# Fixed PSUM banks, whole-bank masked copies and small score products in a linear-attention and feed-forward kernel

## The chip, the cores and the metric

The kernel runs on one core of one Trainium2 chip. The metric is device time in microseconds (us), lower is better. Before the change it is 613.46 us, the median of three runs (613.08 to 613.84). The engines are TensorE (PE, matrix products, with its weight loads PEld), VectorE (DVE), ScalarE (ACT), GpSimd (POOL), and SyncE (SP), which issues DMAs.

## The reference

Two blocks follow each other. The first is a recurrence over time with a decay per channel, for 4 sequences, 8 heads, 768 steps and heads of 48 channels; the second is a feed-forward layer with SiLU from 384 to 2048 and back, on all 3072 tokens, in float32.

```python
for t in range(S):
    cur = np.einsum('bhd,bhe->bhde', u[None] * kt, vt)
    y[:, :, t] = np.einsum('bhd,bhde->bhe', rt, state + cur)
    state = wt[:, :, :, None] * state + np.einsum('bhd,bhe->bhde', kt, vt)
...
x = y.transpose(0, 2, 1, 3).reshape(B * S, H * D)
h = x @ w_in
out = (h * (1.0 / (1.0 + np.exp(-h)))) @ w_out
```

## The kernel before

The work is cut into 12 units: 6 pieces of 128 time steps, each for two pairs of sequences. Within a unit the recurrence is done as scores: a lower triangular matrix of 128 x 128 per head and sequence, which multiplies the values. The triangle is filled in seven levels, l = 0 to 6. At level l, blocks of c = 2^l steps meet in pairs, and the later block of a pair reads the earlier one. Queries (`tr`) and keys (`tk`) are multiplied by decay products between levels: `grow_queries` (L607, on DVE) and `grow_keys` (L625, on POOL), with copies by `odd_keys` (L595, on ACT). From unit 2 on, `prepare` makes a second `tr` (L762 and L764), so that two levels can be multiplied in one go by `burst`. The diagonal comes from `bonus` steps (L430 to L447, later L487 and L521), which are written into `score` by L584 or L557.

A level's products, `score_products`, exist in two forms. The whole form (L694) multiplies, for each of four head pairs p and two heads e, all 128 key steps with the 128 query entries of the level, of which only some lie inside blocks. The small form (L686) multiplies only the parts that are needed: 64 x 64, for level 5 32 x 32. Products with e = 0 and e = 1 go to two PSUM tiles. `keep_masked` (L704) then copies a whole tile of 128 x 512 into `score` under a mask; for small products `keep_level` copies pieces, under masks on DVE (L792, 64 x 128 each, eight a level) or, for levels 5 and 6, plainly (L785), where the first half of level 6 is done by DVE and the rest by ACT. In `scores`, used by units 0 and 1 and by two levels of unit 2, some halves are copied by ACT (L723).

Small products are used from unit 2 on, for levels from `APART` = 3 up. Units 4 and later begin at level 2 with the bonus work on blocks of eight steps, so they multiply only levels 3 to 6; unit 3 has levels 1 to 6.

[...]

After the scores, `turn_apart` (L812) and `turn_k` (L820) turn the keys back, `y_state` (L836) and `y_values` (L844; L857 in units 0 and 1) multiply state and scores into y, L849 copies it out, and `update` (L871, L885) advances the state. The feed-forward layer of a unit runs one or two units later: `up` (L979) in eight groups, each followed by the SiLU on ACT (L988, result `gt`), `sums` (L1027, on DVE) and seven products `quarter` (L1045), each evicted by L1052 or L1054. For units 0 and partly 1, `down` (L1001) is used. In the first 100 us the weights are also rounded, in pieces that pass ACT (L209, L211, L217), DVE (L228, L229) and POOL (L241).

The order is written by hand. Each engine executes its instructions in the order in which the lists of steps at the end of the kernel issue them: units 0 and 1 level by level with the weight pieces between, unit 2 in four lists, and units 3 to 11 by the groups of `mix`, with steps of the feed-forward layer put between groups.

Of the kernel before, what the change touches and what calls it, by code (L numbers as in the profile page):

```python
# [8 lines left out]
F32 = mybir.dt.float32  # L9
# [29 lines left out]
def kernel(  # L39
# [11 lines left out]
    nc = tc.nc  # L51

    B, H, S, D = r.shape
    DM, DF = moe_w_in.shape
    L = 128
    NL = 7
    NB = 2
    NP = H // 2
# [17 lines left out]
    pt = ctx.enter_context(tc.tile_pool(name="pt", bufs=2))  # L76
    ps = ctx.enter_context(tc.tile_pool(name="ps", bufs=1, space=bass.MemoryType.PSUM))
    ctx.enter_context(tc.manual_schedule())


    raw = const.tile([128, NSLOT, 3, NB, H, PD], F32, name="raw")
# [283 lines left out]
    def turn_in(i, s, name):  # L365

        flat = raw[:, i % NSLOT, WRK[name]].rearrange("p b h d -> p (b h d)")
        p_tr = ps.tile([128, NP, NB, L // 2], F32, name="p_m", bufs=2)
        for p in range(NP):
            for e in range(2):  # L370
                at = ((2 * p + e) * 2 + s) * D
                nc.tensor.matmul(p_tr[PD * e:PD * e + PD, p].rearrange("p b i -> p (b i)"), lhsT=flat[:, at:at + PD],
                                 rhs=ident, start=(p == 0), stop=(p == NP - 1))
        turned[i, s, name] = p_tr
# [21 lines left out]
    def reverse_v(i):  # L396
        flat = vq[i].rearrange("p h d -> p (h d)")
        if i < NTOK:
            p_v = ps.tile([128, H * D], F32, name="p_m", bufs=2)
            nc.tensor.matmul(p_v, lhsT=mirror, rhs=flat, start=True, stop=True)  # L400
            nc.scalar.copy(out=flat, in_=p_v)
            return
        nc.vector.stream_shuffle(out=flat, in_=flat, mask=list(range(31, -1, -1)))
# [157 lines left out]
    def bonus_spread(i):  # L561

        if i < NTOK:
            if i == 0:
                diag[i] = p_w[:, 0, 0:NB * H * 2].rearrange("p (b h s) -> p b h s", b=NB, h=H)
            else:
                diag[i] = ps.tile([128, NB, H, 2], F32, name="p_m", bufs=2)
            for b in range(NB):
                for s in range(2):
                    nc.tensor.matmul(diag[i][:, b].rearrange("p h s -> p (h s)"), lhsT=spread[:, s, b, :],  # L570
                                     rhs=own_sums[:, s].rearrange("p h s -> p (h s)"), start=(b == 0 and s == 0),
                                     stop=(b == NB - 1 and s == 1))
            return
        both_b = pt.tile([128, NB, H, 2], F32, name="both_b", bufs=1)
        nc.scalar.copy(out=both_b[:, 0], in_=diag[i][0])
        for g in range(4):
            nc.scalar.copy(out=both_b[(3 - g) * 32:(4 - g) * 32, 1], in_=diag[i][1][g * 32:(g + 1) * 32])
        nc.vector.stream_shuffle(out=both_b[:, 1], in_=both_b[:, 1], mask=list(range(31, -1, -1)))
        diag[i] = both_b
# [76 lines left out]
        start_keys(i, nc.gpsimd, False)  # L656


    APART = FIRST

    def dims_of(have, start, *dims):
        return bass.AP(tensor=have.tensor, offset=have.offset + start, ap=[have.ap[0], *dims])

# [5 lines left out]

    def score_products(i, l, queries, sc):  # L670
        c, ni = 1 << l, L >> (l + 1)
        if i >= NTOK and l >= APART:
            for p in range(NP):
                for x in range(4 if c == 32 else 2):
                    for e in range(2):
                        rows = slice(PD * e, PD * e + D)
                        if c >= 32:
                            b, first = corner(l, x)
                            q = (p, 2 * NP - 1 - p)[b]
                            to, have = sc[e][x * c:(x + 1) * c, q, first // 2 * c:(first // 2 + 1) * c], queries[rows, q, (first + 1) * c:(first + 2) * c]  # L680
                        else:
                            apart = 2 * (NP - p) - 1
                            to = dims_of(sc[e][x * 64:(x + 1) * 64, p, :], 32 * x, [apart * L // 2 + 32 - 64 * x, 2], [1, 32])
                            have = dims_of(queries[rows, p, :], 64 * x + c, [apart * L + 64 - 128 * x, 2], [2 * c, 32 // c], [1, c])
                        m = 32 if c == 32 else 64
                        nc.tensor.matmul(to, lhsT=tk[i][rows, X[l % 2] + p, x * m:(x + 1) * m], rhs=have, start=True, stop=True)  # L686
            return
# [19 lines left out]
    def scores(i, l, *between):  # L707
        c, ni = 1 << l, L >> (l + 1)

        name = "p_h" if i == 0 and l % 2 == 1 else "p_sc"  # L710
        sc = [ps.tile([128, Q, L // 2], F32, name=name, bufs=2) for e in range(2)]
        score_products(i, l, tr[i], sc)
        if i < NTOK and l + 2 < NL:
            odd_keys(i, l + 1)
# [52 lines left out]

    def burst(i, l):

        other = (second[0], "p_o") if i == NTOK else (ps, "p_m")  # L770
        for x, (pool, name) in enumerate(((ps, "p_sc"), other)):
            made[i, l + x] = [pool.tile([128, Q, L // 2], F32, name=name, bufs=2) for e in range(2)]
        score_products(i, l, before.pop((i, l)), made[i, l])
        score_products(i, l + 1, tr[i], made[i, l + 1])

    def keep_level(i, l):
        c = 1 << l
        for e in range(2):
            if l < APART:
                keep_masked(i, l, e, made[i, l])  # L780
                continue
            for x in range(4 if c == 32 else 2):
                if c >= 32:
                    b, first = corner(l, x)
                    (nc.vector.tensor_copy if (l, e) == (NL - 1, 0) else nc.scalar.copy)(  # L785
                        out=score[x * c:(x + 1) * c, i % NSC, e, b * NP:(b + 1) * NP, (first + 1) * c:(first + 2) * c],
                        in_=made[i, l][e][x * c:(x + 1) * c, b * NP:(b + 1) * NP, first // 2 * c:(first // 2 + 1) * c])
                    continue
# [16 lines left out]

    def turn_apart(i):

        apart[i] = [ps.tile([128, NB, NP, D], F32, name="p_sc" if i < NTOK else "p_m", bufs=2) for e in range(2)]
        for x in range(Q):
            for e, to in enumerate(apart[i]):  # L810
                rows = slice(PD * e, PD * e + D)
# [15 lines left out]
    def y_state(i):  # L827

        n, b0 = units[i]
        for e in range(2):  # L830
            p_yt[i, e] = ps.tile([128, NP, L], F32, name="p_m", bufs=2)
        for p in range(NP):
            for b in range(NB):
                for e in range(2):
# [15 lines left out]

    def y(i, b):

        p_yt[i, b] = ps.tile([128, NP, L], F32, name="p_h" if i == 0 else "p_m", bufs=2)
        for p in range(NP):
            for e in range(2):
                h = 2 * p + e
# [6 lines left out]
    def update(i, b):  # L863
# [1 line left out]
        if n == S // L - 1:  # L865
            return
        if b == 0:
            p_kv[i] = ps.tile([128, NB, NP, D], F32, name="p_m" if i < NTOK else "p_sc", bufs=2)
        for p in range(NP):
            for e in range(2):  # L870
                nc.tensor.matmul(p_kv[i][PD * e:PD * e + D, b, p, :], lhsT=kq[i, b][:, p, PD * e:PD * e + D],  # L871
# [17 lines left out]
    def dense_x(i, b):  # L889

        if b == 0:
            xt[i] = pt.tile([128, KC, TU], F32, name="xt", bufs=1)
        p_x = ps.tile([128, KC, L], F32, name="p_h" if i == 0 else "p_m", bufs=2)
        for x, (c, p) in enumerate(parts):
            nc.tensor.matmul(p_x[:, c, :], lhsT=dense[:, x, :], rhs=yt[i][:, p, b, :],
                             start=(x == 0), stop=(x == len(parts) - 1))
# [99 lines left out]
    def down(i, b, part, parts=4):  # L996
        n, b0 = units[i]
        if part == 0:
            po[i, b] = ps.tile([128, DM], F32, name="p_m", bufs=2)
        for f in range(part * FC // parts, (part + 1) * FC // parts):  # L1000
            nc.tensor.matmul(po[i, b], lhsT=gt[i, f // 2][:, f % 2, b * L:(b + 1) * L], rhs=w_out_sb[:, f, :],  # L1001
                             start=(f == 0), stop=(f == FC - 1))
# [72 lines left out]

    def beat(n):

        p = ps.tile([128, L], F32, name="p_m", bufs=2)
        for x in range(n):
            nc.tensor.transpose(p, ident, ident)  # L1080

# [108 lines left out]
```

## Time and profile before

| | |
|---|---|
| median of three runs | 613.46 us |
| profiled execution | 613.64 us |
| its span, first to last instruction | 611.9 us |
| PE busy | 597.9 us (98%) |
| DVE busy | 441.6 us (72%) |
| POOL busy | 361.3 us (59%) |
| ACT busy | 226.2 us (37%) |
| L694, whole products | 256 instructions, 272 ns each at the median |
| L686, small products | 1600 instructions, 211 to 218 ns each at the median |
| L704, masked copy of a whole tile | 29, 690 to 729 ns each at the median |
| L792, masked copy of a piece | 160, 290 to 294 ns each at the median |
| L785 on DVE / on ACT, half of level 6 in pieces of 64 x 256 | 20 of 0.42 us / 20 of 0.37 us |

The busy rows add up each engine's instructions; the span is 1.7 us shorter than the time of the execution. Each product in float32 shows as two instructions. Products overlap within PE, so what a level costs PE is read from the starts of what comes before and after, not from the duration of one instruction. A line of waits names who waited for whom, with total, count and longest in us. In lists by time the first two columns are start and duration; a bracket at the end gives idle time of that engine before the instruction and who ended it. A line by stretch gives, for each engine, busy time and instruction count.

### The profile page before, as it was taken

How to read it: one execution, taken by the hardware profiler on the slowest of the kernel's cores; microseconds unless marked ns; L12 is line 12 of the kernel's file. 1: busy time of each engine (PE TensorE's matmuls, PEld its weight loads, DVE VectorE, ACT ScalarE, POOL GpSimd, SP SyncE). 2: the span in 40 equal slices, each digit the busy share in tenths (PEclk: the TensorE clock that was granted, in tenths of full speed). 3: DMA queues.
4: the chain of work that ended last, by engine and by line, in shares of the span. 5: the costliest groups of instructions: out<-in, count | busy, mean ns of one | idle time of the engine just before them, and what ended most of it. 6: DMA issues, size and time to landing. Idle time of an engine off the chain costs nothing.

```text
span 611.9 us, 14906 instructions
## 1 busy us (share of the span) xinstructions
PE 597.9 (98%) x5790; PEld 534.0 (87%) x5790; DVE 441.6 (72%) x849; ACT 226.2 (37%) x496; POOL 361.3 (59%) x414
## 2 busy tenths in 40 slices
PE   9999999999998998999999999999999999999997
PEld 8788876698798888889889889989989989989997
DVE  7879779899795697687687687587678677761041
ACT  6788883331430440351351341241241242241110
POOL 6998478556578278378478468558658648500000
PEclk9999999999999999999999999999999999999999
DMA  9967773353543643543543552453362322101000
GB/s 225 291 142 196 147 226 46 55 115 49 120 64 52 129 67 55 122 70 53 116 74 54 108 83 51 92 98 53 71 118 51 54 74 53 35 2 27 27 0 27
DMA packets 203079, 53.43 MB, mean 87 GB/s; under 512 B 186752, under 2 KB 194816, under 8 KB 203008
## 3 DMA queue, kind: packets, MB, share of 16 engines
q1 hardware_dynamic: 201424, 51.88, 41.4%
q8 instruction: 46, 0.75, 0.5%
q10 hardware_dynamic: 1584, 0.59, 0.4%
q14 instruction: 25, 0.20, 0.1%
HBM read 43.21 MB, written 5.24 MB: 79 GB/s over the span
## 4 chain that ended last, share of the span: by engine, by line
PE 76%; DVE 9%; SPq 3%; POOL 3%; DMA 3%; issue 2%; ACT 2%; POOLq 0%; DVEq 0%; ACTq 0%
PE p_h L979 35%; PE p_o L1045 28%; SPq L109 3%; DMA tokens_w<-in_w_dram 2%; PE p_m L844 2%; DVE temps L1027 2%; PE p_sc L686 2%; POOL tk L625 2%; PE p_sc L694 2%; PE p_m L1001 1%; PE p_m L686 1%; DVE tr L607 1%; PE p_m L836 1%; DVE score L792 1%; DVE block_sums L521 1%
## 5 line engine op out<-in xcount | busy, mean ns | idle before, releaser
L979 PE MATMUL p_h<-xt,w_in_sb 128*128 128x256 f32 x1152 | 258.9, 382 | 1.8 <-ACT gt L988 1.1
L979 PEld LDWEIGHTS p_h<-xt,w_in_sb 128*128 128x128 f32 x1152 | 215.9, 190 | 33.2 <-ACT gt L988 1.2
L988 ACT ACTIVATE gt<-p_h 128x512 f32<-128x512 f32 x90 | 53.6, 596 | 194.3 <-PE p_h L979 194.0
L625 POOL TENSOR_TENSOR tk<-tk,tw 128x256 f32<-128x256 f32 x128 | 89.9, 724 | 49.1 <-issue 22.9
L1045 PE MATMUL p_o<-own,temps 128*128 128x192 f32 x528 | 88.9, 327 | 4.8 <-DVE temps L1054 4.8
L1045 PEld LDWEIGHTS p_o<-own,temps 128*128 128x128 f32 x528 | 85.9, 190 | 6.2 <-DVE temps L1054 6.0
L1045 PE MATMUL p_o<-w_out_sb,gt 128*128 128x192 f32 x508 | 87.4, 328 | 0.0
L1045 PEld LDWEIGHTS p_o<-w_out_sb,gt 128*128 128x128 f32 x508 | 82.7, 190 | 0.9 <-issue 0.4
L487 POOL TENSOR_TENSOR ruk<-tokens_rk 128x768 f32<-128x768 f32 (+1 forms) x32 | 48.1, 1512 | 52.7 <-DMA tokens_rk<-in_k_dram 40.1
L1027 DVE TENSOR_TENSOR temps<-gt 128x256 f32<-128x256 f32 x84 | 57.5, 684 | 19.8 <-ACT gt L988 19.8
L408 POOL TENSOR_TENSOR tw<-tw 128x256 f32<-128x256 f32 (+6 forms) x83 | 43.9, 529 | 37.2 <-DVE tw L360 33.3
L595 ACT COPY tk<-tk 128x256 f32<-128x256 f32 x52 | 21.0, 403 | 101.5 <-POOL tk L625 72.2
L607 DVE TENSOR_TENSOR tr<-tr,tw 128x512 f32<-128x512 f32 x61 | 52.5, 860 | 4.3 <-POOL tk L625 1.0
L1054 DVE TENSOR_TENSOR partial<-p_o,partial 128x192 f32<-128x192 f32 x33 | 11.8, 356 | 35.7 <-PE p_o L1045 35.3
L1027 DVE TENSOR_TENSOR temps<-temps,gt 128x256 f32<-128x256 f32 x43 | 31.3, 729 | 1.5
L1054 DVE TENSOR_TENSOR temps<-p_o,partial 128x192 f32<-128x192 f32 x22 | 7.9, 358 | 32.2 <-PE p_o L1045 22.7
L1045 PE MATMUL p_o<-w_out_sb,temps 128*128 128x192 f32 x176 | 30.4, 326 | 0.0
L1045 PEld LDWEIGHTS p_o<-w_out_sb,temps 128*128 128x128 f32 x176 | 28.9, 190 | 0.0
L849 ACT COPY yt<-p_m 48x512 f32<-48x512 f32 x40 | 23.2, 580 | 14.9 <-DMA raw<-in_k_dram 7.2
L487 POOL TENSOR_TENSOR spare<-tokens_rk 128x384 f32<-128x384 f32 (+1 forms) x16 | 28.5, 1783 | 0.0
L521 DVE TENSOR_REDUCE block_sums<-ruk 128x4 f32<-128x192 f32 (+1 forms) x48 | 24.1, 542 | 3.6 <-POOL ruk L487 3.6
L634 POOL TENSOR_TENSOR tk<-tk,tw 128x256 f32<-128x256 f32 x32 | 26.2, 839 | 0.0
(186 smaller groups left out, 864.1 us busy)
## 6 DMA issues: line engine op xcount, KB each, us to landing
w_out_sb<-in_moe_w_in_dram SPq DMA_DIRECT2D x6, 768.0 KB, 7.8
w_out_sb<-in_moe_w_out_dram SPq DMA_DIRECT2D x4, 768.0 KB, 5.5
own<-in_moe_w_out_dram SPq DMA_DIRECT2D x4, 768.0 KB, 5.9
tokens_rk<-in_r_dram SPq DMA_DIRECT2D x8, 384.0 KB, 4.5
tokens_rk<-in_k_dram SPq DMA_DIRECT2D x8, 384.0 KB, 5.4
tokens_w<-in_w_dram SPq DMA_DIRECT2D x8, 384.0 KB, 6.3
xt<-yt SPq DMA_DIRECT2D x60, 48.0 KB, 2.0
raw<-in_w_dram SPq DMA_DIRECT2D x80, 32.0 KB, 2.4
```

The costliest lines, as they stand in the source:

```text
L408: engine.tensor_tensor(out=up, in0=t[:, :, 0::2], in1=t[:, :, 1::2], op=ALU.mult)
L487: mul = lambda out, one, two: nc.gpsimd.tensor_tensor(out=out, in0=one, in1=two, op=ALU.mult)
L521: add = lambda out, have: nc.vector.tensor_reduce(out=out, in_=have, axis=mybir.AxisListType.X, op=ALU.add)
L595: nc.scalar.copy(out=keys(i, X[(l + 1) % 2] * L + c, [4 * c, blocks], [c, 2], [1, c]), in_=keys(i, NP * L + c, [4 * c, blocks], [NP * L + ...
L607: nc.vector.tensor_tensor(out=odd, in0=odd, in1=tw[i][l][:, :, 0::2][:, :, :, None].to_broadcast([128, Q, L >> (l + 1), c]), op=ALU.mult)
L625: nc.gpsimd.tensor_tensor(out=out, in0=have, in1=odd_products(i, l, b, *blocks), op=ALU.mult)
L634: nc.gpsimd.tensor_tensor(out=have, in0=have, in1=odd_products(i, l, b, [2, NP * ni]), op=ALU.mult)
L849: nc.scalar.copy(out=yt[i][PD * e:PD * e + D, :, b, :], in_=p_yt[i, e][PD * b:PD * b + D])
L979: nc.tensor.matmul(p_h[:, a, :], lhsT=w_in_sb[:, c, f * 128:(f + 1) * 128], rhs=xt[i][:, c, :], start=(c == 0), stop=(c == KC - 1))
L988: nc.scalar.activation(out=gt[i, m], in_=p_h, func=AF.Silu)
L1027: nc.vector.tensor_tensor(out=out, in0=one, in1=two, op=op)
L1045: nc.tensor.matmul(p, lhsT=left(f), rhs=right[:, f, :], start=(f == 0), stop=(f == FH - 1))
```

## The change

1. `p_m` and `p_sc` are no longer asked from the pool at each use: two tiles of a whole bank each are made once, and a function `bank` hands them out in turn, with the shape that the user wants.
2. Small products are used wherever the unit is not the first (`i > 0`), at all levels, and at level 6 of the first unit.
3. Because a kept bank holds defined data in every place, masked copies may read a whole bank though only parts were just written. So `keep_level` uses `keep_masked` for level 3 and, after unit 2, for level 4 (and 1 and 2 as before). Level 4 of unit 2, whose products lie in `p_o`, keeps the pieces.
4. The first half of level 6 is copied by ACT in place of DVE.

```diff
+    banks = {name: [ps.tile([128, 512], F32, name=f"{name}{x}") for x in range(2)] for name in ("p_m", "p_sc")}
+    turns_of = {name: 0 for name in banks}
+
+    def bank(name, *dims):
+        have = banks[name][turns_of[name] % 2][:]
+        turns_of[name] += 1
+        steps, n = [], 1
+        for d in dims[::-1]:
+            steps.insert(0, [n, d])
+            n *= d
+        return bass.AP(tensor=have.tensor, offset=have.offset, ap=[have.ap[0], *steps])
...
-            p_v = ps.tile([128, H * D], F32, name="p_m", bufs=2)
+            p_v = bank("p_m", H * D)
...
-    APART = FIRST
...
     def score_products(i, l, queries, sc):
         c, ni = 1 << l, L >> (l + 1)
-        if i >= NTOK and l >= APART:
+        if i > 0 or l == NL - 1:
...
-        name = "p_h" if i == 0 and l % 2 == 1 else "p_sc"
-        sc = [ps.tile([128, Q, L // 2], F32, name=name, bufs=2) for e in range(2)]
+        odd = i == 0 and l % 2 == 1
+        sc = [ps.tile([128, Q, L // 2], F32, name="p_h", bufs=2) if odd else bank("p_sc", Q, L // 2) for e in range(2)]
...
     def burst(i, l):
-        other = (second[0], "p_o") if i == NTOK else (ps, "p_m")
-        for x, (pool, name) in enumerate(((ps, "p_sc"), other)):
-            made[i, l + x] = [pool.tile([128, Q, L // 2], F32, name=name, bufs=2) for e in range(2)]
+        made[i, l] = [bank("p_sc", Q, L // 2) for e in range(2)]
+        made[i, l + 1] = [second[0].tile([128, Q, L // 2], F32, name="p_o", bufs=2) if i == NTOK else bank("p_m", Q, L // 2) for e in range(2)]
...
     def keep_level(i, l):
         c = 1 << l
         for e in range(2):
-            if l < APART:
+            if c < 32 and (i > NTOK or l == FIRST):
                 keep_masked(i, l, e, made[i, l])
                 continue
             for x in range(4 if c == 32 else 2):
                 if c >= 32:
                     b, first = corner(l, x)
-                    (nc.vector.tensor_copy if (l, e) == (NL - 1, 0) else nc.scalar.copy)(
+                    nc.scalar.copy(
```

The other uses of `p_m` and `p_sc` change as `p_v` does.

## The prediction

> **What bounds the kernel now.** I read the page first, then busy time by stretches, the waits of PE, and the timeline around each place that the change touches. The busy row:
>
> ```profile
> PE 597.9 (98%) x5790; PEld 534.0 (87%) x5790; DVE 441.6 (72%) x849; ACT 226.2 (37%) x496; POOL 361.3 (59%) x414
> ```
>
> PE works for 597.9 of 611.9 us, so time taken from PE counts unless another engine takes its place at that spot. Busy time by stretches, columns PE, PEld, DVE, ACT, POOL, shows where that is near:
>
> ```profile
> 36.40:66.00 29.60, 29.53 (x226) 24.42 (x227) 26.27 (x33) 27.32 (x41) 25.33 (x28) 1.00 0.65 167
> 66.00:100.00 34.00, 34.00 (x242) 27.32 (x240) 26.49 (x32) 25.53 (x38) 22.00 (x21) 1.00 0.71 173
> 100.00:149.00 49.00, 47.17 (x524) 38.74 (x524) 46.15 (x79) 13.76 (x35) 32.79 (x34) 1.00 0.41 71
> 149.00:190.00 41.00, 38.15 (x406) 33.99 (x397) 36.38 (x67) 13.48 (x34) 26.83 (x30) 1.00 0.44 83
> 190.00:240.00 50.00, 47.88 (x490) 43.57 (x489) 37.60 (x72) 14.70 (x36) 32.09 (x38) 1.00 0.45 81
> 240.00:550.00 310.00, 309.03 (x3174) 280.92 (x3174) 228.84 (x467) 98.09 (x242) 193.40 (x221) 1.00 0.39 71
> ```
>
> From 36 to 66 (unit 1's levels, woven with unit 0's first layer) all engines are nearly full; from 100 to 149 DVE is full 46.15 of 49; after 240 PE has no gap to speak of. Where PE stood idle:
>
> ```profile
> PE p_o L1045 <- DVE temps L1054: 4.8, 4, 2.1
> ...
> PE p_o L686 <- DVE tr L762: 1.1, 1, 1.1
> PE p_h L979 <- ACT gt L988: 1.1, 1, 1.1
> ...
> PE p_m L694 <- POOL tk L625: 0.7, 1, 0.7
> ```
>
> The four waits of L1045 are at 187 (1.76), 236 (2.12), 374 (0.38) and 423 (0.59). The other three are at 116, 162 and 139.
>
> [...] A whole level and a pair of small levels:
>
> ```profile
> 50.05 1.16 PE L694 MATMUL p_sc<-tr,tk 48*128 48x128 f32 x16
> 51.14 2.86 PE L979 MATMUL p_h<-xt,w_in_sb 128*128 128x256 f32 x12
> ```
> ```profile
> 148.38 0.69 PE L686 MATMUL p_sc<-tr,tk 48*64 48x64 f32 x32
> 148.89 0.65 PE L686 MATMUL p_m<-tr,tk 48*64 48x64 f32 x32
> 149.47 10.63 PE L979 MATMUL p_h<-xt,w_in_sb 128*128 128x256 f32 x48
> ```
>
> Start to start, the whole level holds PE for 51.14 - 50.05 = 1.09 us with 16 instructions; two small ones hold it for 149.47 - 148.38 = 1.09, the first 0.51, the second, with the change back to a full array, 0.58.
> [...]
> [...]
>
> **The change, part by part.**
> (a) *Kept banks.* The names p_m and p_sc alternate between two tiles as before, in the same order of users. Before, a new tile waits until all users of the one two turns back are done; now the first writer waits for the bank's last readers, which are the same instructions. Cost taken: 0. The bounds: 0 to 0.1 us a level, by one or two more 51 ns waits; that end is the slower rival below.
>
> (b) *Small products* in unit 1, levels 1 to 6; unit 2, levels 1 and 2; unit 3, levels 1 and 2; unit 0, level 6. A single small level between full-array work: 0.46 (the first of the pair up to its last weight load, 148.37 to 148.83) plus 0.17 for the two changes of mode, by the pair's 1.09 = 2 x 0.46 + 0.17: 0.63, saves 0.46. Level 5 with its 64 instructions starts at 160.02 and is followed at 160.71: 0.69, saves 0.40. On PE that is 9 x 0.46 + 0.40 = 4.5 us, unit 0 apart. What arrives:
> Unit 0's level 6 (27.35): the chain there runs over the DVE's L584, ACT's p_w and POOL, not PE: 0.
> Unit 1: each level's products need the two banks that DVE copies out of for the level below, and DVE runs without a gap from 40.84 to 60.66. Level 1: lost, since level 2 waits for the copy that ends at 46.06 anyhow. From there PE alone, with shorter levels (0.63, 2.79 per L979 group, the small steps L871, L570 and L400 as they are), reaches level 3 at 49.95 (copy done 49.80), level 4 at 54.2, level 5 at 59.2 and level 6 at 62.7. DVE waited 0.84 us at 60.66 for level 5's products; that wait goes, so the copy for level 5 ends at 63.61 - 0.84 = 62.77 and level 6 starts at about 62.95 in place of 64.08: 1.13, and its own 0.46: **1.6 us** earlier at 66. Bounds 0.9 (DVE's wait alone) to 2.2 (no DVE limit).
> From 66 to 91 ACT, DVE and POOL waited for PE at the start (ACT 2.04 at 68.06, POOL 4.68 at 68.86, DVE 2.62 at 71.35), so all move by 1.6.
> Unit 2, levels 1 and 2: PE gains 0.9 more, but DVE runs without a gap from 91.31 to 116.2 and PE waits for it at 116.36: 0.
>
> (c) *Masked copies of whole banks*, levels 3 (unit 2 on) and 4 (unit 3 on): eight pieces at a pitch of 0.26, 2.06 us, become two copies of 128x512. L704 shows 1.31 for two, 2.44 when POOL's work falls on them: -0.75 to +0.4 a level. At level 3 of unit 2 (109.08) it lies on the DVE run to 116.36; between the bounds I take **0.4**. In units 3 on DVE has gaps after it (6.4 of 10 busy at 200 to 210), and PE waits for none of it: 0.
> Unit 3's level 1 at 137.40: its gain only lengthens the 0.70 wait for POOL at 139.29. Level 2 at 139.29 counts: **0.46**.
>
> (d) *Level 6, first half, from DVE to ACT*: 20 DVE copies of 0.42 leave, 20 ACT copies of 0.37 come. [...] On DVE 0.86 us leave ahead of the run that ends at L1054. At 236 (run from 213.74) part is lost, as POOL's four L487 from 214.33 let one DVE operation through at a time: 0.4 to 0.86, taken **0.6**; at 374 and 423 PE's waits are shorter than that: **0.38** and **0.59**. At 187 it gives nothing: DVE waited for gt at 166.62, which ACT does after the level 6 copies, now 0.74 longer, while (c) lets the bonus chain (L437, POOL L430, L432, L441, the diag transfer) that delays ACT at 162 start 0 to 0.7 sooner: net 0, bounds -0.6 to +0.5. A shorter wait at 162 becomes a longer one at 187.
>
> Sum: 1.6 + 0.4 + 0.46 + 0.6 + 0.38 + 0.59 = 4.0 us. The profiled execution took 613.64 us, span 611.9 and 1.74 around it; so 607.9 of span and 609.6. The median, 613.46, is 0.18 lower: **609.4 us**.
>
> **The rivals.**
> *Others take it back*: in 36 to 66 only DVE's 0.84 us arrives, or the copies at 109 are blocked by POOL (-0.4), and the runs before 236, 374 and 423 gain half (0.8). 0.84 - 0.4 + 0.46 + 0.8 = 1.7: 611.8. For it: DVE 26.27, ACT 27.32 of 29.6 in that stretch. Against it: PE's waits on DVE are few and short after 240.
> *All arrives*: the 4.5 us of PE work and half of the 7 us of gaps between 100 and 430: 8.0, so 605.5. Against it: the DVE runs to 116 and 187, which nothing shortens by that much.
> *Slower: waits per piece.* Kept banks could make each small product carry its own wait for the copy that read its part, instead of one for the bank. After the change 51 levels are small (1, 6, 6, 6 and 8 x 4); each extra wait holds PE's queue 51 ns, 2.6 us over all. It decides from 1.5 extra waits a level (4.0 / 51 = 0.08 us); with three, 7.8 - 4.0: 617.3. [...]
>
> **How the numbers follow.** Chances: the forecast 0.58, own range 607.5 to 611.2 (the low ends 0.9, 0, -0.6 and 0.4 above, against the high ends 2.2 and 0.75); taken back 0.20 (611.2 to 613.2); all arrives 0.10 (604.5 to 607.5); slower 0.12. Leaving out the slower case and most of "all arrives" gives 606.5 to 613.2. Differences up to 0.2%, 1.2 us, are about what this kernel's measurement can't tell from none: faster 0.80 (a part, 0.12, of "taken back" included), same 0.08, slower 0.12.
>
> **What would show it.** Small products at unit 1 to 3 with a period near 0.63; L979 of unit 0's group 7 starting near 63.6 instead of 65.17; y_values of unit 2 near 122.2 instead of 124.20; no L1045 wait left at 374 and 423, one near 1.5 at 236, one still near 1.8 at 187; queue waits at the small products no more than about two a level. It is wrong if DVE's run from 40.84 stays the limit for level 6, if two whole copies take 2.4 in most units, or if level 6's ACT copies show up as waits of L979 for L988.

## The result and the profile after

The changed kernel takes 612.41 us (median), measured beside the kernel before at 614.49: a ratio of 0.9957, with a 95% interval of 0.994 to 0.9974. (Every ratio here is the estimate that comes with such an interval, not the quotient of the two medians, which would be 0.9966.) A second measurement, in another comparison further down, gave 0.9965 (0.9948 to 0.9982). On the 613.46 that the prediction started from, 0.9957 is 610.8 us (609.8 to 611.9): 2.6 us faster (1.6 to 3.7) where 4.0 were forecast. The profiled execution took 611.3 us, with a span of 609.5, against 611.9 before.

The busy row of the page, after:

```profile
PE 594.1 (97%) x5998; PEld 530.7 (87%) x5998; DVE 423.8 (70%) x715; ACT 232.7 (38%) x516; POOL 367.2 (60%) x414
```

Busy time on PE fell by 3.8 us and on DVE by 17.8, yet the span fell by 2.4: PE is idle for longer than before (15.4 us of the span against 14.0). Busy time by stretches, with the same stretches and columns as before; after the five engines come PE's granted clock, the share of DMA and GB/s:

```profile
36.40:66.00 29.60, 27.97 (x360) 22.87 (x359) 27.01 (x35) 26.56 (x41) 24.93 (x27) 1.00 0.63 165
100.00:149.00 49.00, 46.22 (x579) 38.51 (x578) 45.92 (x72) 14.60 (x37) 31.68 (x35) 1.00 0.43 72
149.00:190.00 41.00, 39.78 (x386) 35.94 (x385) 31.92 (x54) 15.14 (x38) 30.46 (x37) 1.00 0.43 83
190.00:240.00 50.00, 46.67 (x472) 42.27 (x471) 33.89 (x54) 15.15 (x38) 31.17 (x36) 0.97 0.45 80
240.00:550.00 310.00, 310.00 (x3195) 282.13 (x3194) 219.04 (x370) 103.51 (x258) 196.44 (x216) 1.00 0.39 71
```

Two stretches are new in kind. In 36 to 66, PE had almost no gap before (0.07 us) and has 1.63 us of gaps now. In 190 to 240 PE has 3.33 us of gaps in place of 2.12, and its clock is 0.97 on average. In 149 to 190 DVE has 4.46 us less to do (36.38 before), and PE gained 1.6. Where PE stood idle:

```profile
PE p_o L1056 <- DVE temps L1065: 4.5, 2, 3.3
PE p_sc L698 <- DVE tr L621: 1.6, 1, 1.6
...
PE p_h L990 <- POOL w_in_sb L255: 1.1, 1, 1.1
...
```

(L1056 was L1045, L698 L686, L990 L979. `p_h` takes mostly the first layer's products, `p_o` the second's, `p_sc` scores and state updates, and `p_m` most of the rest.) The wait for `gt` at 162 is gone, so are those of 0.38 and 0.59 at 374 and 423. The one before unit 4's `quarter` grew from 2.12 to 3.33, the one of 1.13 at 116 (unit 2's level 6) became one of 1.56 at 114, ahead of level 5, and a new one of 1.05 stands in unit 1's stage.

To say where the time went, I cut each profiled execution at four starts that every kernel has: unit 1's first level, unit 3's first level, unit 4's level 5, and unit 5's level 3. The rows below the first two are a repeat and experiments, told further down. All times are in us, from starts of score products in the timeline of PE; the last column is the mean granted clock of that execution.

| kernel | to unit 1 | to unit 3 | to unit 4's level 5 | to unit 5 | to the end | span | clock |
|---|---|---|---|---|---|---|---|
| before | 39.21 | 98.19 | 74.77 | 34.51 | 365.22 | 611.9 | 0.999 |
| changed | 38.75 | 97.14 | 72.36 | 37.46 | 363.79 | 609.5 | 0.997 |
| changed, again | 39.05 | 98.77 | 71.57 | 36.97 | 363.64 | 610.0 | 0.994 |
| kept banks alone | 39.29 | 98.57 | 74.15 | 35.77 | 363.72 | 611.5 | 0.999 |
| small products alone | 38.81 | 98.44 | 73.44 | 38.44 | 364.47 | 613.6 | 0.997 |
| copies alone | 38.77 | 97.89 | 72.80 | 36.07 | 363.77 | 609.3 | 0.997 |
| changed, pieces | 39.03 | 98.94 | 72.96 | 36.11 | 364.16 | 611.2 | 0.994 |
| changed, level 6 on DVE | 38.85 | 100.44 | 71.15 | 35.87 | 364.39 | 610.7 | 0.996 |
| before, loads moved | 38.91 | 98.21 | 74.74 | 32.13 | 365.81 | 609.8 | 0.999 |
| changed, loads moved | 38.91 | 97.17 | 72.42 | 32.12 | 365.08 | 605.7 | 1.000 |
| the same, again | 39.35 | 98.82 | 71.96 | 32.13 | 365.34 | 607.6 | 0.997 |
| copies alone, loads moved | 39.44 | 97.91 | 73.19 | 32.13 | 364.63 | 607.3 | 1.000 |
| small products alone, loads moved | 39.35 | 98.91 | 72.72 | 32.23 | 367.29 | 610.5 | 0.997 |
| changed, loads moved, filler | 38.85 | 97.36 | 73.07 | 32.12 | 365.40 | 606.8 | 0.999 |

The first column differs between executions of the same kernel (38.75 to 39.35 in the four profiles of the changed kernel with and without the move told below), so 0.46 of the 2.4 us may be no more than that. Then -1.05, -2.41, +2.95 and -1.43. So 3.46 us had been gained between units 1 and 4, and most of it was given back in one place, the stage around 233.

**That place.** The timeline of DVE, after. Column one is the start, column two the duration, and the bracket is the engine's idle time before it with who ended it:

```profile
209.13 0.01 DVE L565 LOAD_MASK_SELECT spare<-spare  x1 [8.03 <-ACT spare L564]
...
209.39 2.50 DVE L571 COPY_PREDICATED score<-spare 128x1024 f32<-128x1024 int8 x2
```

This is the head of the DVE run whose end (L1065, 233.02 and 233.30) releases PE. DVE stood idle for 8.03 us ahead of it. The same place in the kernel before:

```profile
210.95 0.01 DVE L551 LOAD_MASK_SELECT spare<-spare  x1 [4.28 <-ACT spare L550]
...
211.21 2.50 DVE L557 COPY_PREDICATED score<-spare 128x1024 f32<-128x1024 int8 x2
```

PE had come 3.92 us forward by level 5, this run only 1.82. (The run itself became 0.83 us shorter, 23.63 against 24.46 us up to L1065's start. So 2.12 + 3.92 - 1.82 - 0.83 = 3.39 us is the wait to be expected, and 3.33 is what the trace has.) The run waits for the diagonal blocks: `block_sums` is written out to `kept` by one DMA and read back into `spare` by two more. The timeline of SP's queue shows what these stand behind:

```profile
188.81 9.12 SPq L123 DMA_DIRECT2D raw<-in_r_dram  x16
198.03 3.85 SPq L123 DMA_DIRECT2D raw<-in_w_dram  x8
...
203.28 0.33 SPq L554 DMA_DIRECT2D kept<-block_sums  x1
205.30 1.00 SPq L557 DMA_DIRECT2D spare<-kept  x2
```

The sums were ready at 197.76 (the end of L535), 5.5 us before their store was issued (in the kernel before at 202.59, 2.5 us before it). Ahead of the store were 24 loads of raw data, and the next instructions of DVE that read such data are the transposes at 220.03 (L374). PE's end of the story:

```profile
227.35 2.76 PE L1056 MATMUL p_o<-own,temps 128*128 128x192 f32 x16
233.43 7.15 PE L1056 MATMUL p_o<-own,temps 128*128 128x192 f32 x32 [3.33 <-DVE temps L1065]
```

The 32 products took 7.15 us, where the same 32 took 5.47 at 183: the clock is 0.83 on average in 230 to 240. The wait and the lower clock after it cost 1.2 and 1.7 us more than in the execution before, 2.9 of the 2.95.

### The profile page after: what moved, and what is told of

Same layout as the page of the kernel before. It is cut to its first block, busy times and chain, and to the rows that moved or that the text cites. A ratio compares the mean times of both kernels' runs of the same rounds, so it can differ in the third digit from the quotient of the medians.

```text
span 609.5 us, 15190 instructions
## 1 busy us (share of the span) xinstructions
PE 594.1 (97%) x5998; PEld 530.7 (87%) x5998; DVE 423.8 (70%) x715; ACT 232.7 (38%) x516; POOL 367.2 (60%) x414
## 4 chain that ended last, share of the span: by engine, by line
PE 72%; DVE 12%; DMA 4%; POOL 3%; ACT 3%; issue 3%; SPq 3%; DVEq 0%; POOLq 0%; ACTq 0%
PE p_h L990 31%; PE p_o L1056 30%; PE p_m L855 2%; DVE score L716 2%; DVE temps L1038 2%; DVE tr L621 2%; SPq L123 2%; PE p_sc L698 2%; POOL tk L639 2%; PE p_m L698 1%; DMA raw<-in_w_dram 1%; PE p_m L847 1%; DMA tokens_w<-in_w_dram 1%; DVE p_w L242 1%; DMA raw<-in_r_dram 1%
## 5 line engine op out<-in xcount | busy, mean ns | idle before, releaser
L990 PE MATMUL p_h<-xt,w_in_sb 128*128 128x256 f32 x1152 | 258.9, 382 | 1.8 <-POOL w_in_sb L255 1.1
L990 PEld LDWEIGHTS p_h<-xt,w_in_sb 128*128 128x128 f32 x1152 | 215.9, 190 | 32.8 <-POOL w_in_sb L255 1.2
L639 POOL TENSOR_TENSOR tk<-tk,tw 128x256 f32<-128x256 f32 x128 | 93.7, 753 | 43.5 <-issue 22.9
L1056 PE MATMUL p_o<-own,temps 128*128 128x192 f32 x528 | 90.2, 331 | 4.5 <-DVE temps L1065 4.5
L1056 PEld LDWEIGHTS p_o<-own,temps 128*128 128x128 f32 x528 | 87.6, 193 | 5.4 <-DVE temps L1065 5.3
L1056 PE MATMUL p_o<-w_out_sb,gt 128*128 128x192 f32 x508 | 87.4, 328 | 0.0
L1056 PEld LDWEIGHTS p_o<-w_out_sb,gt 128*128 128x128 f32 x508 | 82.7, 190 | 0.9 <-issue 0.4
L501 POOL TENSOR_TENSOR ruk<-tokens_rk 128x768 f32<-128x768 f32 (+1 forms) x32 | 50.0, 1573 | 52.0 <-DMA tokens_rk<-in_k_dram 31.9
L621 DVE TENSOR_TENSOR tr<-tr,tw 128x512 f32<-128x512 f32 x61 | 56.4, 924 | 15.3 <-PE p_m L698 12.4
L1065 DVE TENSOR_TENSOR partial<-p_o,partial 128x192 f32<-128x192 f32 x33 | 11.8, 358 | 38.9 <-PE p_o L1056 38.7
L716 DVE COPY_PREDICATED score<-mask,p_sc 128x512 f32<-128x512 int8 x42 | 31.1, 795 | 2.7 <-PE p_sc L698 2.5
L1056 PE MATMUL p_o<-w_out_sb,temps 128*128 128x192 f32 x176 | 30.4, 326 | 0.0
L1065 DVE TENSOR_TENSOR temps<-p_o,partial 128x192 f32<-128x192 f32 x22 | 7.9, 357 | 31.9 <-PE p_o L1056 22.4
L1056 PEld LDWEIGHTS p_o<-w_out_sb,temps 128*128 128x128 f32 x176 | 28.9, 190 | 0.0
L698 PEld LDWEIGHTS p_sc<-tr,tk 48*32 48x32 f32 (+1 forms) x1312 | 18.1, 119 | 11.6 <-issue 6.3
L501 POOL TENSOR_TENSOR spare<-tokens_rk 128x384 f32<-128x384 f32 (+1 forms) x16 | 28.1, 1754 | 0.0
```

The costliest lines, as they stand in the source:

```text
L501: mul = lambda out, one, two: nc.gpsimd.tensor_tensor(out=out, in0=one, in1=two, op=ALU.mult)
L621: nc.vector.tensor_tensor(out=odd, in0=odd, in1=tw[i][l][:, :, 0::2][:, :, :, None].to_broadcast([128, Q, L >> (l + 1), c]), op=ALU.mult)
L639: nc.gpsimd.tensor_tensor(out=out, in0=have, in1=odd_products(i, l, b, *blocks), op=ALU.mult)
L716: nc.vector.copy_predicated(out=dst, mask=masks[l][:, :, None].to_broadcast([128, NB, NP, ni, c]), data=sc[e].rearrange("p (b q) (i c) -> ...
L990: nc.tensor.matmul(p_h[:, a, :], lhsT=w_in_sb[:, c, f * 128:(f + 1) * 128], rhs=xt[i][:, c, :], start=(c == 0), stop=(c == KC - 1))
L1056: nc.tensor.matmul(p, lhsT=left(f), rhs=right[:, f, :], start=(f == 0), stop=(f == FH - 1))
```

## The experiments

My theory after this comparison: what small products save on PE is worth little, because DVE's run in unit 4, and before it the transfer in SP's queue, sets that stage's end; the gain that arrived is DVE's relief by parts (c) and (d). The rival was the prediction's own sum, in which small products bring more than half. A second rival, that kept banks themselves change the order of waits, had to be out of the way first.

**Kept banks alone.** The changed kernel with the three other edits undone:

```diff
-        if i > 0 or l == NL - 1:
+        if i >= NTOK and l >= FIRST:
...
-            if c < 32 and (i > NTOK or l == FIRST):
+            if l < FIRST:
...
-                    nc.scalar.copy(
+                    (nc.vector.tensor_copy if (l, e) == (NL - 1, 0) else nc.scalar.copy)(
```

> Only the kept banks: whole products in units 1 to 3, copies in pieces, half of level 6 on DVE, all as before. My theory: the waits are the same, so the ratio to before is 1.000 within 0.2%, and the queue waits on PE at the score products stay at 68. The rival of waits per piece: over 1.003, with more queue waits of 51 ns.

Measured: ratio 1.0015 (0.9998 to 1.0031). Kept banks cost nothing that shows, or at the very most 0.3%. The queue waits at the score products are 56 here, not the 68 expected: fewer, where the rival needed more. The waits of PE hold a surprise:

```profile
PE p_o L1056 <- DVE temps L1065: 5.1, 2, 3.3
```

One wait of 3.32 at 237, and none at 374 or 423, where the kernel before had 2.12, 0.38 and 0.59, together 3.09. So the two short waits vanish without any relief of DVE in an execution in which PE has waited longer before; it looks like one debt, paid early or late. Their absence in the changed kernel therefore doesn't show that part (d) took them.

**Copies alone** (kept banks, whole-bank copies, level 6 on ACT; products as before):

```diff
-        if i > 0 or l == NL - 1:
+        if i >= NTOK and l >= FIRST:
```

> The changed kernel without the new small products (units 1 to 3 and level 6 of unit 0 as before). If the small products made the start of unit 4's products 3.4 us earlier, as the traces suggest, this kernel reaches them only 1 to 1.5 us earlier than before (by the shorter wait at unit 3's first layer, from the shorter DVE copies). Because PE then meets unit 4's late DVE run less early, its wait there should be near 2 us and no clock drop should follow: total 1.5 to 2.5 us faster than before, so nearly what the full change gives. The rival (all of the gain comes from PE's products): ratio 0.999 to 1.001.

Measured: ratio 0.9964 (0.9946 to 0.9981), the changed kernel's own. Without the new small products nearly the whole gain is there. The expectation had the time right, but not the way to it: unit 4's products start 2.71 us earlier than before (195.22 against 197.93) and not 1 to 1.5, and after the wait, 2.01, the clock did fall, to 0.50 in 234 to 236.

**Whole-bank copies of levels 3 and 4 undone:**

```diff
-            if c < 32 and (i > NTOK or l == FIRST):
+            if l < FIRST:
```

> The changed kernel with copies of levels 3 and 4 in pieces as before. My theory: the wait of PE for the gt activation in unit 3's first layer (1.09 us before, gone after) comes back, since DVE frees the bonus chain later: start of unit 4's products about 1 us later than in the changed kernel. The total then depends on unit 4's wait, which should shrink by as much: within 1 us of the changed kernel. The rival (copies matter through DVE's load everywhere): 2 us slower or more.

Measured: 0.9985 (0.9966 to 1.0004), so these copies are worth about 0.25%, 1.5 us, against the mean of the changed kernel's two ratios, 0.9961; the intervals overlap, so the size is uncertain. It lies between the expectation (within 1 us) and its rival (2 us or more). In its profile 0.6 of that lies in the stretch to unit 4's level 5, where the waits at 161 (0.21, for `gt`) and 186 (1.73 instead of 1.22) are back. The wait for `gt` was expected back at its full 1.09.

**First half of level 6 back on DVE:**

```diff
-                    nc.scalar.copy(
+                    (nc.vector.tensor_copy if (l, e) == (NL - 1, 0) else nc.scalar.copy)(
```

> The changed kernel with the first half of level 6 back on DVE. My theory: DVE's runs start 0.86 us later in each unit, so the waits for L1065 in the units near 374 and 423 (0.38 and 0.59 before) stay, and unit 4's wait grows by 0.86 to over 4 us with the clock drop: 1.5 to 2.5 us slower than the changed kernel. The rival (ACT in place of DVE changes nothing, or delays gt): the same or faster than the changed kernel.

Measured: 0.9986 (0.9971 to 1.0002), about 1.5 us as well, again with intervals that overlap. That is the size expected, but not for the reason given: no wait came back at 374 or 423, and unit 4's wait is 3.33 and not over 4. The profile puts the loss elsewhere than that of the pieces: in unit 2 PE waited 1.32 us at 123 for ACT's `kq` copy, which stood behind two waits of 1.52 and 1.11 us for the diagonal's DMA, and its clock was 0.61 in the four us after that. One profile doesn't show whether that follows from DVE's copies or came by chance.

**Small products alone** (kept banks and small products; pieces, and level 6 on DVE, as before): the second and third edit of the first diff.

> Kept banks and small products alone; the copies of levels 3 and 4 stay in pieces, and the first half of level 6 stays with DVE. Theory: what small products save on PE by unit 3 is taken back by DVE's run in unit 4 and by waits for DVE and POOL before that, so they give nothing or nearly nothing alone: ratio 0.999 to 1.0015. Rival, the prediction's own sum: 1.6 in unit 1 and 0.46 in unit 3, so 2.1 us, ratio 0.9966; with the gain of 0.9 that the trace shows in unit 1 it would be 0.9978.

Measured: 1.0008 (0.9996 to 1.0021). The rival's 0.9966 and 0.9978 both lie outside. Up to unit 4's level 5 the profile is 1.48 us ahead of the kernel before (38.81 + 98.44 + 73.44 = 210.69 against 212.17), and then:

```profile
PE p_o L1056 <- DVE temps L1065: 5.5, 3, 3.3
```

3.33 us of wait at 237, with a low clock after it (0.997 over the execution), and 38.44 us for a stage that the kernel before passes in 34.51.

**The transfer in SP's queue.** Unit 4's loads of raw data were spread over its groups from the second on; now over those from the fifth on, so that the kept blocks are stored and read ahead of more of them. Only the place changes, in one unit:

```diff
-        behind = groups[10 if i < NPAIR else 1:]
+        behind = groups[10 if i < NPAIR else 4 if i == NPAIR else 1:]
```

> The changed kernel, and unit 4's raw loads (24 transfers, issued one after the other on SP's queue at 188.8 to 201.9) moved behind four more groups, so that the store and load of the kept blocks (203.28 in the changed kernel) go ahead of part of them. Theory: at 233 PE waits for a run of DVE whose start (209.39) is set by the kept blocks' transfer, which stands behind 16 + 8 raw loads in SP's queue; moved ahead of the last eight (3.85 us) it comes 2 to 3.9 us earlier, the run of DVE starts that much earlier, PE's wait at 233 (3.33 in the changed kernel) becomes 0 to 1.4, and the time is 2 to 3.5 us below the changed kernel's, a ratio to the kernel before of about 0.990 to 0.993. Rival: DVE's run there is limited by POOL's instructions, which block it, or by its own length; then the start moves and the end does not, the wait stays at 2 to 3.3, and the ratio is that of the changed kernel, 0.9957 within 0.2%.

Measured: 608.95 us, ratio 0.9908 (0.9886 to 0.9931); in a second comparison 609.33 us and 0.9924 (0.9902 to 0.9947). The changed kernel, run again beside the first:

> The changed kernel as it is, to stand beside the three others on the same chip. Every theory expects the ratio measured first, 0.9957 within 0.2%. Its trace shows whether the wait at 233 (3.33) and the lower clock after it (0.83 in the stretch of 230 to 240) come again: by the theory that these are chance from run to run, either may be absent.

Measured: 0.9965 (0.9948 to 0.9982). So the move takes another 0.3 to 0.6% off, 0.45% at the mean of both measurements of each kernel (3.6 us where the two stood side by side, 612.58 to 608.95), and both ratios lie where the theory has them. SP's queue and DVE in the kernel with the move:

```profile
188.59 7.99 SPq L123 DMA_DIRECT2D raw<-in_r_dram  x16
...
198.48 0.40 SPq L554 DMA_DIRECT2D kept<-block_sums  x1
200.24 1.00 SPq L557 DMA_DIRECT2D spare<-kept  x2
...
203.29 11.46 SPq L123 DMA_DIRECT2D raw<-in_w_dram  x16
```
```profile
205.21 0.01 DVE L565 LOAD_MASK_SELECT spare<-spare  x1 [3.85 <-ACT spare L564]
...
209.97 2.06 DVE L621 TENSOR_TENSOR tr<-tr,tw 128x512 f32<-128x512 f32 x1 [2.01 <-PE p_m L698]
```

The store goes out 4.8 us earlier, DVE starts its run at 205.21, and now DVE waits 2.01 us for PE instead of PE for DVE. No wait is left near 231, and the stage takes 32.12 us. That number came out in all kernels with the move (32.12 to 32.23): it is PE's own work there (busy 50.00 of the 50 us from 190 to 240). But a part comes back one unit on:

```profile
277.71 5.47 PE L1056 MATMUL p_o<-own,temps 128*128 128x192 f32 x32 [1.06 <-DVE temps L1065]
```

From 240 on the changed kernel had no wait for DVE at all, since its wait at 233 had given DVE time; this one has 1.06.

**The same move in the kernel before:**

> The kernel before with the same move of unit 4's raw loads alone. Theory: in the kernel before PE was late enough at 212 that the kept blocks arrived just in time (211.21), and the wait at 236 was 2.12; the move takes 0 to 1 us of it: ratio 0.9985 to 1.000. Rival (the transfer is the limit in the kernel before as well): the whole wait of 2.12 goes, ratio 0.9965.

Measured: 0.9982 (0.9967 to 0.9997). This is just beyond the theory's strong end, 0.9985, and the profile decides for the rival's reading: the wait at 236 is gone altogether and the stage takes 32.13. The transfer was the limit in the kernel before too. The rival's size, 0.9965, didn't come: of the 2.4 us saved there 0.6 came back, as waits of 1.09 at 281 and 0.50 at 421, where there had been 0.97 at 374 and 423.

**What are small products worth once the transfer is out of the way?** Two kernels and a repeat, on one chip: copies alone with the move, small products alone with the move, all with the move.

> The changed kernel with the move of unit 4's raw loads, but without the new small products (whole products as in the kernel before). Theory: small products gave nothing in the changed kernel only because the kept blocks' transfer, which stands at a fixed place in SP's queue, set the end of unit 4's run of DVE; with the transfer moved, what PE saves (1 to 2 us at unit 3's end by the traces) arrives, so this kernel is 0.3% slower than the changed kernel with the move: ratio about 0.9935 against 0.9908. Rival: the move alone makes the gain and small products are worth nothing in any case: ratio 0.9908 within 0.2%.

> Kept banks, small products and the move of unit 4's raw loads; copies of levels 3 and 4 in pieces, first half of level 6 with DVE, as in the kernel before. Theory: small products arrive now, 0.3% on top of the move alone (0.9982): ratio about 0.995. Rival: DVE's copies set the time without the relief, and small products still give nothing: 0.998.

> The changed kernel with the move of unit 4's raw loads once more, beside the two others on the same chip: the ratio measured first, 0.9908 within 0.2%, no wait left near 231, and a granted clock of 1.00 in the stretch of 230 to 240.

Measured: 609.45 us and 0.9928 (0.9906 to 0.995); 611.63 and 0.9966 (0.9949 to 0.9983); 609.33 and 0.9924 (0.9902 to 0.9947). All with the move is level with copies alone with the move: the theory's 0.3% doesn't show in this comparison (with the first measurement of all with the move, 0.9908, it would be 0.2%). Against the move alone, 0.9982, small products give 0.16%, and the two intervals overlap. That lies between the theory's 0.995 and the rival's 0.998. So the theory that the transfer alone hid their gain is not borne out. The profiles show four places where it goes. PE saves 5.3 us of busy time (592.4 against 597.7 in the two kernels with the move whose clock was 1.000). In the first stage, unit 1's level 6 does come earlier, but the wait of 1.05 for POOL follows; in unit 2, PE is at level 5 sooner and waits 1.55 us for DVE, in place of 0.90 at level 6; in unit 5 a longer wait at 278 (1.06 and 1.40, against 0.73) takes some of the rest. The last is the clock: in the repeat, the stretch to unit 3 took 98.82 us instead of 97.17, and the clock (0.50 in 116 to 118) is the main thing that differs. Busy time by stretches of two us of the changed kernel's second profile, in which it happened as well:

```profile
116.00:118.00 2.00, 2.00 (x15) 1.60 (x8) 1.93 (x6) 1.93 (x7) 0.00 (x0) 0.50 0.07 10
118.00:120.00 2.00, 2.00 (x9) 1.56 (x7) 0.59 (x1) 0.54 (x2) 0.00 (x0) 0.84 0.07 6
```

The granted clock is 0.50 right after the wait at 114, and 1.6 us are lost (98.77 against 97.14).

**Does the idle time lower the clock?** In the kernel with the move, five transposes whose results are thrown away fill PE's wait ahead of unit 2's level 5:

```diff
         made[i, l + 1] = [second[0].tile(...
+        if (i, l) == (NTOK, 5):
+            for x in range(5):
+                nc.tensor.transpose(made[i, l][1].rearrange("p q l -> p (q l)")[:, 0:L], ident, ident)
```

> The changed kernel with the move of unit 4's raw loads, and five transposes of the identity (work that is thrown away) on PE ahead of unit 2's level 5, where PE waits 1.55 us for DVE at 113. Theory: the idle time there (1.55, then 0.27) is what lowers the granted clock to 0.50 for about 3 us in some executions (two of four of the changed kernels, with and without the move), 1.65 us each time; with PE busy the clock stays 1.00 at 110 to 120, the way from unit 1's first small level to unit 3's is 97.2 rather than 98.8, and the time is about 0.8 us lower than with the move alone at the mean: a ratio of 0.990 to 0.992. Rival: the clock falls for another reason, the transposes only take time that was idle, and half of the executions still lose 1.65: ratio 0.9916, the mean of the two measurements with the move alone.

Measured: 608.22 us, ratio 0.9893 (0.9853 to 0.9934). The clock stayed at 1.00:

```profile
116.00:118.00 2.00, 2.00 (x15) 1.51 (x15) 1.86 (x5) 1.57 (x6) 0.00 (x0) 1.00 0.14 13
118.00:120.00 2.00, 2.00 (x23) 1.79 (x20) 0.00 (x0) 0.71 (x2) 0.00 (x0) 1.00 0.07 6
```

and the stretch to unit 3 took 97.36. That is what the theory says, but by the rival one profile would show the same half of the time. None of the six timed executions with the filler has a lowering (0.999 or 1.000 each), but without it only two of eleven have one, and the intervals of the times overlap. So this stays open. It is the fastest kernel measured, 0.9893, though not shown to be faster than the one without the filler.

Every timed execution has its mean granted clock, and that says more than one profile does. One lowering shows as 0.003 of the mean.

| kernel | executions | mean clock | median us of those at 0.997 | of those at 1.000 |
|---|---|---|---|---|
| before (beside the first four experiments) | 66 | 0.9980 | 614.6 (16) | 613.0 (26) |
| kept banks alone | 22 | 0.9960 | 614.9 (8) | 612.7 (3) |
| copies alone | 21 | 0.9982 | 612.2 (10) | 609.6 (9) |
| small products alone | 22 | 0.9952 | 614.4 (10) | 611.6 (1) |
| changed, pieces | 14 | 0.9959 | 613.3 (4) | 611.9 (1) |
| changed, level 6 on DVE | 22 | 0.9953 | 612.4 (8) | 610.5 (1) |
| changed | 20 | 0.9965 | 611.5 (13) | 608.5 (1) |
| changed, again | 11 | 0.9962 | 612.5 (4) | 610.2 (2) |
| before, loads moved | 22 | 0.9981 | 613.3 (7) | 612.0 (9) |
| small products alone, loads moved | 22 | 0.9970 | 611.8 (12) | 610.0 (4) |
| copies alone, loads moved | 6 | 0.9998 | none | 609.8 (5) |
| changed, loads moved | 5 | 0.9998 | none | 608.8 (4) |
| the same, again | 6 | 0.9987 | 609.3 (2) | 609.3 (2) |
| changed, loads moved, filler | 6 | 0.9995 | none | 607.6 (3) |

At an equal clock the changed kernel is 2.1 to 4.5 us faster than before. The 4.5 rests on a single execution; the other three pairs give 2.1 to 3.1, less than the forecast 4.0. And at an equal clock small products do tend to help: -0.5 and -1.1 (alone, against kept banks alone), -1.5 and -2.0 (with the move), -0.5 and -1.0 (all with the move, against copies with the move), and +0.6 to -1.1 (all, against copies alone). What they may take in exchange is the clock: 0.9965 and 0.9962 with them against 0.9982 without (all, against copies alone), which is 0.0017 to 0.0020 of 610 us, 1.0 to 1.2 us. In the other three pairs the clock is lower with them by 0.0008, 0.0011, and 0 or 0.0011. The groups are small and were not all measured side by side, so these are sizes and not proof, but the two terms together would explain why leaving the small products out changes nothing. Kept banks alone have a low clock as well, 0.9960, and their 0.15% is gone at an equal clock; so small products are not the only thing that goes with a low clock.

## Why the prediction was right and where it was wrong

The median came out 1.4 us above the forecast on the forecast's own base, inside its own range and on its side of no change. But the interval on that base, 609.8 to 611.9, leaves the forecast's 609.4 just outside and holds the 611.8 of the rival "others take it back". And errors of both signs stand behind the sum. For the four stretches of the table after the first, it has 2.0 us (1.6 + 0.4), 0.46, 0.6 and 0.97 (0.38 + 0.59); the changed kernel's first profile has 1.05, 2.41, -2.95 and 1.43, its second -0.58, 3.20, -2.46 and 1.58. Only the last is near in size, and (d) below says that its reason doesn't hold. That the total came out near is in good part luck.

*(a) Kept banks at 0.* Right, by the run that has them alone. Score products carry 56 queue waits in all, 51 ns at the median (52 at L698, 4 at L706), against 68 before (24 at L694, for 16 whole levels, and 44 at L686), so the slower rival, which needed 1.5 extra a level, is refuted by the trace.

*(b) Small products.* The size was right to the hundredth:

```profile
38.75 0.70 PE L698 MATMUL p_sc<-tr,tk 48*64 48x64 f32 x32
39.38 2.86 PE L990 MATMUL p_h<-xt,w_in_sb 128*128 128x256 f32 x12
```

0.63 us start to start, and level 5 is followed after 0.69. Measured is the 0.63 as a whole: that 0.17 of it is the price of two changes of mode is shown by no run; it is what the pair's 1.09 leaves over 2 x 0.46. What failed is "so all move by 1.6". The end of unit 1:

```profile
62.08 0.70 PE L698 MATMUL p_sc<-tr,tk 48*64 48x64 f32 x32
63.83 1.35 PE L990 MATMUL p_h<-xt,w_in_sb 128*128 128x256 f32 x5 [1.05 <-POOL w_in_sb L255]
```

Level 6 comes 2.00 us earlier, 1.54 counted from the stage's start, more than the 1.13 foreseen. Then `up`'s last group waits for its weights, which POOL rounds between 61.95 and 63.77 (L255). That step had DVE's copies as the only limit; the busy view gave POOL 25.33 of 29.6 us in that stretch, and the weights that `up` reads were a second limit. 0.88 arrived (63.83 against 65.17, less the 0.46 of the start).

*(c) Whole-bank copies.* The pair takes 1.3 us in place of 2.06, as foreseen, also at level 3 of unit 2 (1.29 at 108.09). The 0.4 in the sum for that level lies between two bounds, 1.31 and 2.44 us a pair. That POOL's work makes the difference is not shown: before, a pair took 2.47 at 43.59 and 1.31 at 48.49, with POOL at work through both. But "PE waits for none of it: 0", of units 3 on, and "A shorter wait at 162 becomes a longer one at 187" failed, in the good direction. The diagonal of unit 3 is ready for DVE to spread at (before, then after):

```profile
162.00 0.17 DVE L578 STREAM_SHUFFLE both_b<-both_b 128x16 f32<-128x16 f32 x1
```
```profile
157.91 0.17 DVE L592 STREAM_SHUFFLE both_b<-both_b 128x16 f32<-128x16 f32 x1
```

4.1 us earlier, where PE's level 5 moved only 2.2, so 1.9 more. The wait of 1.09 at 162, for a `gt` that ACT does after its copies of the diagonal, is gone, and that at 187 fell from 1.76 to 1.22 (0.99 in the second profile).

Not all of this is (c)'s. The diagonal's DMAs are issued 3.4 us ahead of level 5 in every profile with copies in pieces, and 4.0 to 4.4 ahead in every one with whole-bank copies. That 1.0 is (c)'s: two levels of copies are shorter, and the DVE operation after them is faster (L621 took 1.31 there instead of 2.16). The step allowed 0 to 0.7. The other 0.9 lies in these DMAs themselves: they land within 1.8 us in all nine profiles with small products, and only after up to 2.6 to 3.6 us in the five without. Why is not shown. With copies alone and the loads moved, the wait at 162 is back in spite of (c):

```profile
161.66 8.39 PE L990 MATMUL p_h<-xt,w_in_sb 128*128 128x256 f32 x36 [1.08 <-ACT gt L999]
```

The two waits together are 2.85 to 3.00 us in the three profiles with neither part, 1.94 to 1.98 in the three with small products and pieces, 1.56 and 1.70 in the two with copies alone, and 0.99 to 1.57 in the six with both. So small products by themselves took about 1.0 us of these waits, and copies by themselves 1.3; the sum has neither. Undoing (c) costs about 1.5 us in all, with the uncertainty said above, against 0.4 in the sum.

*(d) Level 6 on ACT.* Undoing it costs about 1.5 us, as the sum's 0.6 + 0.38 + 0.59 = 1.57 has it, but not by those steps; and part of that cost may be clock (0.9953 against 0.9965 and 0.9962). The wait of about 1.5 foreseen at 236 is wrong: 3.33 and 2.90 were left. The copies on ACT don't show as waits of L990 for `gt`: none is left in the changed kernel's first profile. The run of DVE did become shorter, by 0.83 where 0.6 was taken. The 0.6 was an estimate from four operations of DVE at 214.63 to 219.71 that took 2.06, 2.03, 1.11 and 1.23 us, beside POOL's four L487 of 1.81, 2.13, 1.18 and 1.07, where L1027 took 0.41 at 220.86. The changed kernel has four like them at 212.82 to 217.75 (1.92, 2.03, 1.21 and 1.23 beside L501). That POOL's work alone makes them slow is not shown: L607 took 2.06 at 214.63 and 0.68 at 236.21, both beside L487. What the step had wrong is the start: it let DVE's run come forward with PE, and in fact its first instruction waits for a transfer in SP's queue, so that PE's gain up to there (3.46 us, and the start) could not pass. That was to be seen in the trace of before, as DVE's idle time of 4.28 us ahead of L551 and the store of `kept` behind 24 raw loads. And the waits of 0.38 and 0.59 went in the kernel with kept banks alone as well.

*The clock* isn't in the sum at all. The sum holds PE's rate constant, and part of the forecast gain is paid in lower clock after waits that the change makes longer: 1.6 us after that at 114 in the second profile, 1.7 after that at 233 in the first.

Of the rivals, "others take it back" had the right idea, but not its places: the copies at 109 and the runs before 374 and 423 weren't where it was lost. "All arrives" is excluded: its 605.5 would be a ratio of 0.987. (The gaps from which it took half add up to 7.8 us by the waits listed, not 7; and part (c)'s own bound of 0.4 us lost stands as 0 in the low end of the range. Neither changes what was compared.)

## What to carry to other kernels

Before counting work saved on the busiest engine, follow the next long wait back past the engine that ends it, to the head of that engine's run: if the head waits for a DMA, look at what stands ahead of that DMA in its queue, and move first what nobody needs soon. Here one line about unit 4's loads brought about as much on top of the change (0.45% at the mean) as the change itself (0.35 to 0.43%); in the kernel before the same line brought 0.18%. Work taken from an engine that then waits may also cost clock (here a wait of 3.33 us was followed by 32 products that took 7.15 us and not 5.47), so a gap should be removed and not just moved.

## What was unexpected in the hardware

The granted clock fell to 0.50 for some 3 us after waits of 1.24 to 3.3 us. At 114, it fell in four of the eight profiles in which PE had waited 1.24 to 1.57 us there, and in none of six with 1.13 or less; 1.6 to 1.7 us were lost each time. At 233 to 237, it fell in five of eight profiles with waits of 2.0 to 3.3 us, and not in the other three, one of 2.12 and two of 3.3. It fell once more at 125, after the wait of 1.32 with level 6 on DVE (0.61 on average in the four us after 124), and nowhere else in the fourteen profiles. The waits of 0.6 to 1.9 us at 183 to 187, and one of 2.38 at 281, never lowered it. So the length of the wait doesn't decide alone. The shortest wait after which it fell was 1.24 us, with 0.28 more after a short level. In the changed kernel's second profile it was 0.81, 0.50 and 0.84 in three stretches of 2 us from 114 on, 1.7 us lost. What else decides is not shown.
